# First batch of a sparse-attention and expert kernel: an earlier load, one more query buffer, and a conversion cut in two

## Chip, cores, metric

The kernel runs on one core of a Trainium2 chip. The metric is the device time of one execution in microseconds (us). TensorE (PE) multiplies, VectorE (DVE), ScalarE (ACT) and GpSimd (POOL) do the rest, SyncE (SP) issues most of the loads.

## What is computed

Four batches of attention over 768 positions with 8 heads of 64, in blocks of 32 positions. A query block sees its neighbours, the first and the last block and three sampled blocks; the first and last query block see everything. The 3072 rows of the result go through four experts, weighted by token probabilities.

```python
mask = np.abs(blk_i - blk_j) <= 1
mask = mask | (blk_i == 0) | (blk_j == 0) | (blk_i == n_blocks - 1) | (blk_j == n_blocks - 1)
...
    mask[qb * block:(qb + 1) * block, kb * block:(kb + 1) * block] = True   # sampled blocks
attn = softmax(where(mask, q @ k.T / 8, -1e9)) ; x = attn @ v      # 4 x 8 x 768 x 64
...
p = domain_probs / (domain_probs.sum(-1, keepdims=True) + 1e-09)
for e in range(E):                                                 # 4 experts, 512 -> 1024 -> 512
    h = np.maximum(x @ w1[e], 0.0)
    out += p[:, e:e + 1] * (h @ w2[e])
```

## The kernel before, in words

**Attention units.** A batch is 16 units (`units`, L378): four `Edge` units for the first and last query block, and twelve `Group` units, two for each of six groups of four query blocks (the last group has two blocks). A unit has four steps. `S` computes scores on TensorE, their maxima on VectorE (L266 or L332) and the exponentials on ScalarE (L269 or L337). `T` transposes the probabilities on TensorE (L278) and copies them back on ScalarE (L280). `A` multiplies them with the values (L291) and scales the result on VectorE (L297 to L299). `X`, for the second unit of a group, transposes the result once more (L310) and copies it into the tokens `xr` (L312).

**Loads.** `load_batch` brings keys, `load_q` (L98) the queries of a group, `load_v` (L124) its values (four loads on SyncE, four indirect ones on GpSimd). `copy_k` (L113) copies the edge blocks and the three sampled key blocks of each query block, on GpSimd, ScalarE and VectorE in turn. In the first batch queries have two buffers, values six, which hold the batch's own two tiles and two groups' four.

**The first batch** (loop at L643) is written out by hand, and every engine keeps the order of the program. Step n issues `S` of unit n, `X` of unit n-3, `A` of unit n-2 and `T` of unit n-1; from step 5 on, every second step also issues the loads and copies of the next group but one. Step 9 issues `token_weights` (L619: the load of the expert probabilities, then four small VectorE operations that normalise them) and the first expert weights. From step 11 on each step also takes one piece of weight preparation (`operands`, L446: ScalarE casts to a rounded high part at L464, GpSimd subtracts for the low part at L465), and steps 12 to 15 split a tile of the second weights (L480, L481).

**Conversion.** The expert product works with seven combinations of token quarters, each as a high part (ScalarE cast, L392) and a low part (subtraction on VectorE or GpSimd, L393). `conversion` (L401) makes them in the order 2, 1, 5, 6, 3, 7, 4; four of them need a subtraction on VectorE first (L407, L410, L415, L418). In the first batch 2 and 1 (columns 0 to 383, complete by then) are made at step 12, the five others after the last unit, one ahead of each of the first expert products (L605).

**Expert stream.** `first` (L494) multiplies one combination with a piece of the first weights, six matmuls into PSUM: products 2, 1, 5, 6, 3, 7, 4 in turn, of which 1, 6, 7 and 4 accumulate in one PSUM tile `w` and the others use one tile `v`. ScalarE and VectorE combine the results (L522 to L539). `second` (L542) does the second layer. In the later batches the units are spread through this stream.

Of the kernel before, what the change touches and what calls it, by code (L numbers as in the profile page):

```python
# [8 lines left out]
F32 = mybir.dt.float32  # L9
F32R = mybir.dt.float32r  # L10
# [7 lines left out]
P = 128  # L18
BLOCK = 32
# [4 lines left out]
def attention_moe_kernel(ctx: ExitStack, tc, qb, kb, vr, sampled, sampled_t, probs, w1, w2, out):  # L24


    nc = tc.nc
# [9 lines left out]
    HS = S // 2  # L37
    KH = DM // P // 2
# [5 lines left out]
    QG = P // BLOCK  # L44
    NG = (NB - 2 + QG - 1) // QG
# [4 lines left out]
    xp = ctx.enter_context(tc.tile_pool(name="xp", bufs=1))  # L50
    wp = ctx.enter_context(tc.tile_pool(name="wp", bufs=4))
    at = ctx.enter_context(tc.tile_pool(name="at", bufs=2))
    gp = ctx.enter_context(tc.tile_pool(name="gp", bufs=2))
    ps_at = ctx.enter_context(ExitStack())
    pool = {"s": ps_at.enter_context(tc.tile_pool(name="ps_s", bufs=4, space=PSUM)),
            "a": ps_at.enter_context(tc.tile_pool(name="ps_a", bufs=2, space=PSUM)),
            "o": ps_at.enter_context(tc.tile_pool(name="ps_o", bufs=2, space=PSUM))}
    setup = ctx.enter_context(ExitStack())
    p1 = setup.enter_context(tc.tile_pool(name="p1", bufs=1))
    pool["v"] = setup.enter_context(tc.tile_pool(name="v1", bufs=6))  # L60
    pool["k"] = setup.enter_context(tc.tile_pool(name="k1", bufs=8))

    def f32(ap):
        return ap.bitcast(F32)
# [30 lines left out]
    def blocks(t):  # L95
        return range(1 + QG * t, min(1 + QG * (t + 1), NB - 1))

    def load_q(b, t):  # L98
        js = blocks(t)
        q = gp.tile([P, QG, P], F32, name="q")  # L100
        nc.sync.dma_start(q[:, :len(js)], qb[b, :, js[0]:js[-1] + 1])
        gathered[b, t] = q, {}, {}

# [3 lines left out]
    def sampled_block(j, r):  # L107
        if (j, r) not in regs:
            regs[j, r] = COPIERS[r % len(COPIERS)].value_load(sbrow[:1, j * NR + r, :1],
                                                              min_val=0, max_val=NB - 1)  # L110
        return regs[j, r]

    def copy_k(b, t, cs=range(QG)):  # L113
        for c, j in enumerate(blocks(t)):
            if c in cs:
                k = pool["k"].tile([P, SLOTS - 3, P], F32, name="kr")
                nc.gpsimd.tensor_copy(k[:, :2], keys[b][0][:, 0:NB:NB - 1])
                for r in range(NR):
                    eng = COPIERS[r % len(COPIERS)]
                    copy = eng.copy if eng is nc.scalar else eng.tensor_copy  # L120
                    copy(k[:, 2 + r:3 + r], keys[b][0][:, bass.ds(sampled_block(j, r), 1)])
                gathered[b, t][1][c] = k
# [71 lines left out]
    for r in range(1, NR):  # L194
        for e in range(r):
# [20 lines left out]
    nc.tensor.matmul(mps.rearrange("p t n -> p (t n)"), ind4, sel.rearrange("p t n -> p (t n)"),  # L216
                     start=True, stop=True)
    nc.vector.tensor_copy(mask, mps)

    xr = {}
# [152 lines left out]
    later = {}  # L375
# [11 lines left out]

    xo = {}

    def split(n, src, eng):  # L390
        o = xo[n] = (xp if n in (1, 2) else later["x"]).tile([P, 2, KH, HS], F32R, name=f"xo{n}")
        nc.scalar.copy(o[:, 0], src)  # L392
        eng.tensor_sub(o[:, 1], src, f32(o[:, 0]))  # L393

    def token_blocks(b):
        return [xr[b][:, k * KH:(k + 1) * KH, g * HS:(g + 1) * HS] for k in range(2) for g in range(2)]

    def conversion(b):


        b11, b12, b21, b22 = (xr[b][:, k * KH:(k + 1) * KH, g * HS:(g + 1) * HS]  # L401
                              for k in range(2) for g in range(2))
        split(2, b21, nc.gpsimd)
        yield
        split(1, b11, nc.vector)
        yield
        nc.vector.tensor_sub(b11, b12, b11)  # L407
        split(5, b11, nc.vector)
        yield
        nc.vector.tensor_sub(b11, b22, b11)  # L410
        split(6, b11, nc.vector)
        yield
        split(3, b22, nc.gpsimd)
        yield
        nc.vector.tensor_sub(b12, b22, b12)  # L415
        split(7, b12, nc.vector)
        yield
        nc.vector.tensor_sub(b21, b21, b11)  # L418
        split(4, b21, nc.gpsimd)
        xr.pop(b)  # L420
        yield

    pieces = {}

    def convert(b):
        if b in pieces:
            next(pieces[b], None)
# [188 lines left out]
    pr = const.tile([P, NT // P, E], F32, name="pr")  # L616
    psum_e = const.tile([P, NT // P], F32, name="psum_e")

    def token_weights():  # L619
        nc.sync.dma_start(pr, probs)  # L620
        nc.vector.reduce_sum(psum_e, pr, axis=AX.X)
        nc.vector.tensor_scalar(psum_e, psum_e, 1e-9, None, op0=ALU.add)
        nc.vector.reciprocal(psum_e, psum_e)
        nc.vector.tensor_mul(pr, pr, psum_e.unsqueeze(2).broadcast_to([P, NT // P, E]))
# [3 lines left out]


    with ExitStack() as only:  # L630
        pool["p"] = only.enter_context(tc.tile_pool(name="pp1", bufs=3))
        pool["pt"] = only.enter_context(tc.tile_pool(name="pt1", bufs=2))
        pool["copy"] = nc.vector.tensor_copy
        pool["tag"] = "o"
        pool["xg"] = 1
        load_batch(0)
        load_q(0, 0)
        load_v(0, 0)
        copy_k(0, 0)
        us = units(0)  # L640
        N = len(us)
        E0 = N - 2 * NG
        for n in range(N + 3):  # L643
            if n < N:
                us[n].S()
            if 0 <= n - 3 < N:
                us[n - 3].X()
            if 0 <= n - 2 < N:
                us[n - 2].A()
            if 0 <= n - 1 < N:  # L650
                us[n - 1].T(0)
                us[n - 1].T(1)
            if n == 1:
                load_q(0, 1)
                load_v(0, 1)
                copy_k(0, 1)
            t = (n - E0) // 2
            if n >= E0 and n % 2 and t + 2 < NG:
                load_q(0, t + 2)
                load_v(0, t + 2)  # L660
                copy_k(0, t + 2)

            if n == N - 7:
                token_weights()
                for s in range(2):
                    load_w1(0, s)
                    load_w2(s)
            if n == N - 4:
                pieces[0] = conversion(0)
                convert(0)  # L670
                convert(0)
            if N - 5 <= n < N + 2:
                next(weights)
            if N - 4 <= n < N:
                split_w2(n - N + 4)
# [2 lines left out]
    pool["a"] = pool["o"] = ctx.enter_context(tc.tile_pool(name="ps_a2", bufs=1, space=PSUM))  # L678
    later["m"] = ctx.enter_context(tc.tile_pool(name="ps_m2", bufs=1, space=PSUM))
    setup.close()  # L680
    later["x"] = ctx.enter_context(tc.tile_pool(name="xp2", bufs=1))
    pool["v"] = ctx.enter_context(tc.tile_pool(name="v2", bufs=3))
    pool["k"] = ctx.enter_context(tc.tile_pool(name="k2", bufs=5))
    pool["p"] = ctx.enter_context(tc.tile_pool(name="pp2", bufs=1))
# [3 lines left out]
    later["h"] = ctx.enter_context(tc.tile_pool(name="hp", bufs=2 * FT))  # L688
    later["c"] = ctx.enter_context(tc.tile_pool(name="cp", bufs=2))
    later["o"] = ctx.enter_context(tc.tile_pool(name="op", bufs=KT))  # L690
    convert(0)
    LEAD, TAIL = 12.0, 25.0
    for b in range(1, B):
# [5 lines left out]
        for n in range(N + 1):  # L699
# [12 lines left out]
            if n == 1:  # L712
                copy_k(b, 0)
                load_v(b, 0, (0, 1))
            t = (n - E0 + 2) // 2
            if n % 2 == 0 and 0 < t < NG:
# [54 lines left out]
```

## Time and profile before

| | |
|---|---|
| three runs, us | 1334.69, 1330.58, 1332.21 (median 1332.21) |
| profiled execution, us | 1331.5 |
| its span (first to last instruction), us | 1329.8 |
| mean granted TensorE clock | 0.983 |
| busy share: PE, DVE, ACT, POOL | 94%, 57%, 48%, 51% |
| DMA, mean over the span | 106 GB/s |

A busy share is an average over the whole span; the change touches only the first 120 us of it. The views below are by stretch or in order of time, counted from the span's start. "Idle before, releaser" names the last event that an engine waited for; "issue" stands where the profile shows none. PEclk 1.00 is TensorE's upper level, 2.4 GHz, 0.50 the lower, 1.2 GHz.

### The profile page before, as it was taken

To read this page: it belongs to the slowest core of one execution; us is meant where nothing else is said; L and a number is where in the kernel's file an instruction comes from. 1 tells how busy PE (TensorE), PEld (TensorE's weight loads), DVE (VectorE), ACT (ScalarE), POOL (GpSimd) and SP (SyncE) were. 2 spreads that over 40 slices of the span, in tenths; PEclk is the share of its full clock that TensorE was granted. 3 is DMA by queue.
4 is the path that set the end of the run, shared out by engine and by line. 5 is a ranking of instruction groups with operands and counts; after the bars stand their busy time and mean duration, and the time that the engine had idled before them with its cause. 6 is when DMAs were issued, how large, how long until landed. Compare 5 with 4: busy or idle time off the path is not lost.

```text
span 1329.8 us, 31410 instructions
## 1 busy us (share of the span) xinstructions
PE 1255.4 (94%) x12238; PEld 1079.0 (81%) x12238; DVE 755.5 (57%) x1750; ACT 642.3 (48%) x1678; POOL 675.9 (51%) x872
## 2 busy tenths in 40 slices
PE   7677999999998999999999799999999989999998
PEld 4456888888886778888887688888888778888887
DVE  5476655555556556556545755556555665555553
ACT  4474455555543455555553444555554444444441
POOL 5544555566435455655544543665553464444451
PEclk9898999999998999999999999999999999999999
DMA  8832233353233233444414221444431222222111
GB/s 252 248 117 107 90 96 121 111 151 109 89 112 118 68 96 104 125 128 124 132 62 157 95 72 56 144 122 135 120 107 50 88 79 72 64 64 64 64 48 64
DMA packets 60050, 140.51 MB, mean 106 GB/s; under 512 B 7163, under 2 KB 8700, under 8 KB 59900
## 3 DMA queue, kind: packets, MB, share of 16 engines
q1 hardware_dynamic: 52816, 115.41, 27.6%
q0 software_dynamic: 7040, 23.07, 6.2%
q8 instruction: 96, 1.57, 0.5%
q14 instruction: 54, 0.44, 0.1%
q10 hardware_dynamic: 44, 0.00, 0.0%
HBM read 132.17 MB, written 6.29 MB: 104 GB/s over the span
## 4 chain that ended last, share of the span: by engine, by line
PE 82%; DVE 7%; ACT 4%; DMA 3%; issue 2%; POOL 1%; SPq 1%; DVEq 0%; ACTq 0%
PE po L550 36%; PE w L502 19%; PE v L502 14%; PE o L291 4%; PE tp L278 3%; DMA r<-in_w_dram 2%; PE s L256 2%; PE sw L325 1%; DVE hl L510 1%; PE s L251 1%; DVE oacc L565 1%; DVE xo L393 1%; PE ow L356 1%; ACT hh L509 1%; ACT xo L392 1%
## 5 line engine op out<-in xcount | busy, mean ns | idle before, releaser
L465 POOL TENSOR_TENSOR wo<-r,wo 128x256 fp32r<-128x256 f32 x384 | 301.8, 788 | 411.1 <-ACT wo L464 410.5
L502 PE MATMUL w<-xo,wo 128*128 128x384 f32 x1536 | 316.8, 342 | 14.9 <-DVE z L536 10.9
L550 PE MATMUL po<-h,hh 128*128 128x512 f32 x768 | 312.7, 407 | 7.7 <-DVE oacc L565 7.7
L502 PEld LDWEIGHTS w<-xo,wo 128*128 128x128 f32 x1536 | 276.4, 190 | 39.9 <-DVE z L536 10.9
L550 PE MATMUL po<-h,hl 128*128 128x512 f32 x768 | 305.7, 398 | 0.0
L550 PE MATMUL po<-l,hh 128*128 128x512 f32 x768 | 305.5, 398 | 0.0
L502 PE MATMUL v<-xo,wo 128*128 128x384 f32 x1152 | 238.6, 343 | 12.1 <-ACT p L522 7.9
L464 ACT CAST wo<-r 128x256 fp32r<-128x256 f32 x384 | 153.4, 400 | 181.8 <-DVE r L459 102.9
L502 PEld LDWEIGHTS v<-xo,wo 128*128 128x128 f32 x1152 | 206.8, 190 | 29.3 <-ACT p L522 9.2
L481 POOL TENSOR_TENSOR l<-r,h 128x512 fp32r<-128x512 f32 x128 | 167.6, 1310 | 44.3 <-ACT h L480 44.3
L550 PEld LDWEIGHTS po<-h,hl 128*128 128x128 f32 x768 | 145.4, 189 | 34.0
L550 PEld LDWEIGHTS po<-h,hh 128*128 128x128 f32 x768 | 145.7, 190 | 28.9 <-DVE oacc L565 9.8
L550 PEld LDWEIGHTS po<-l,hh 128*128 128x128 f32 x768 | 146.0, 190 | 14.4
L524 DVE TENSOR_TENSOR p<-w,p 128x384 f32<-128x384 f32 x64 | 35.7, 558 | 166.7 <-PE w L502 163.9
L565 DVE SCALAR_TENSOR_TENSOR oacc<-po,pr,oacc 128x512 f32<-128x512 f32 x168 | 120.3, 744 | 8.1 <-PE po L550 8.0
L269 ACT ACTIVATE p<-p,mx 128x256 f32<-128x256 f32 (+1 forms) x192 | 95.4, 498 | 49.3 <-DVE mx L266 49.3
L136 POOL DMA_INDIRECT v<-in_vr_dram,vidx x88 | 85.0, 966 | 59.4 <-PE o L291 28.4
L465 POOL TENSOR_TENSOR wo<-s,wo 128x256 fp32r<-128x256 f32 x64 | 48.4, 755 | 105.2 <-ACT wo L464 105.2
L266 DVE CUSTOM_DVE_ANT_1 p<-s,mask 128x256 f32<-128x256 f32 (+1 forms) x192 | 69.9, 419 | 56.0 <-PE s L256 56.0
L480 ACT CAST h<-r 128x512 fp32r<-128x512 f32 x128 | 79.2, 619 | 23.0 <-PE po L550 11.6
L510 DVE SCALAR_TENSOR_TENSOR hl<-z,hh 128x384 fp32r<-128x384 f32 x64 | 56.7, 887 | 39.4 <-ACT hh L509 39.4
L509 ACT ACTIVATE hh<-p 128x384 fp32r<-128x384 f32 x64 | 33.6, 525 | 87.5 <-DVE p L524 87.5
(113 smaller groups left out, 1450.5 us busy)
## 6 DMA issues: line engine op xcount, KB each, us to landing
r<-in_w_dram SPq DMA_DIRECT2D x64, 512.0 KB, 3.7
r<-in_w_dram SPq DMA_DIRECT2D x128, 256.0 KB, 2.6
v<-in_vr_dram SPq DMA_DIRECT2D x44, 384.0 KB, 4.7
k<-in_kb_dram SPq DMA_DIRECT2D x8, 768.0 KB, 5.4
out_dram<-oacc SPq DMA_DIRECT2D x24, 256.0 KB, 2.0
v<-in_vr_dram SPq DMA_DIRECT2D x44, 128.0 KB, 4.5
q<-in_qb_dram SPq DMA_DIRECT2D x20, 256.0 KB, 4.1
v<-in_vr_dram SPq DMA_DIRECT2D x4, 1024.0 KB, 9.1
```

The lines of the kernel that those rows point to most:

```text
L136: nc.gpsimd.indirect_dma_start(out=v[:, i, 1], out_offset=None, in_=vr, element_offset=b * S * DM, in_offset=bass.IndirectOffsetOnAxis(ap= ...
L266: nc.vector.tensor_tensor_reduce(p.rearrange("p (a b) -> p a b", b=BLOCK), s[h][:n, i], mk, -SCALE, 3.0e38, ALU.add, ALU.min, mx[:n])
L269: nc.scalar.activation(p, p, AF.Exp, bias=mx[:n], scale=-1.0, accum_out=self.sums[:n, m:m + 1])
L291: nc.tensor.matmul(o[cs, m], self.pt[:, 2 * m + k, cs], vs[c][:, k, e], start=k == 0, stop=k == 1)
L464: nc.scalar.copy(o[:, 0], src)
L465: nc.gpsimd.tensor_sub(o[:, 1], src, f32(o[:, 0]))
L480: nc.scalar.copy(h, r)
L481: nc.gpsimd.tensor_sub(l, r, f32(h))
L502: nc.tensor.matmul(ps, w[:, wi, t], x[:, xi, t], start=fresh and m == 0, stop=m == 3 * KH - 1, skip_group_check=not fresh)
L510: nc.vector.scalar_tensor_tensor(hl, src, 0.0, f32(hh), op0=ALU.max, op1=ALU.subtract)
L550: nc.tensor.matmul(p, a[:, js], w, start=f == 0 and n == 0, stop=f == FT - 1 and n == 2)
L565: nc.vector.scalar_tensor_tensor(accs[tok], p, pe, accs[tok], op0=ALU.mult, op1=ALU.add)
```

## The change

Six edits, all for the first batch. (1) The load of the expert probabilities moves from step 9 to step 3; the normalising operations stay at step 9. (2) Queries get three buffers in the first batch (two afterwards, as before). (3) The block copies of group 0 move behind the scores of unit 0. (4) Probability tiles of the first batch have two buffers instead of three. (5) Combinations 5, 6, 3, 7 and 4 are converted in two parts: columns 0 to 287 of their 384 in steps 16 to 18, right behind `X`, `A` and `T` of the step, and columns 288 to 383 where the whole stood. (6) The memory of the mask tiles is freed once the mask is made, and all `xo` tiles stand in one pool from the start.

```diff
+    pool["q"] = setup.enter_context(tc.tile_pool(name="q1", bufs=3))
+    masks = setup.enter_context(ExitStack())
+    p1 = masks.enter_context(tc.tile_pool(name="p1", bufs=1))
...
-        q = gp.tile([P, QG, P], F32, name="q")
+        q = pool["q"].tile([P, QG, P], F32, name="q")
...
+    masks.close()
...
-    def split(n, src, eng):
-        o = xo[n] = (xp if n in (1, 2) else later["x"]).tile([P, 2, KH, HS], F32R, name=f"xo{n}")
+    def split(n, src, eng, lo=0, hi=HS):
+        if lo == 0:
+            xo[n] = xp.tile([P, 2, KH, HS], F32R, name=f"xo{n}")
+        o = xo[n][:, :, :, lo:hi]
         nc.scalar.copy(o[:, 0], src)
         eng.tensor_sub(o[:, 1], src, f32(o[:, 0]))
...
+    def conversion_early(b):
+        b11, _, b21, _ = halves(b)
         split(2, b21, nc.gpsimd)
         yield
         split(1, b11, nc.vector)
         yield
+    def conversion_late(b, lo=0, hi=HS):
+        b11, b12, b21, b22 = halves(b, lo, hi)
         nc.vector.tensor_sub(b11, b12, b11)
-        split(5, b11, nc.vector)
+        split(5, b11, nc.vector, lo, hi)
...
     def token_weights():
-        nc.sync.dma_start(pr, probs)
...
-        pool["p"] = only.enter_context(tc.tile_pool(name="pp1", bufs=3))
+        pool["p"] = only.enter_context(tc.tile_pool(name="pp1", bufs=2))
...
-        copy_k(0, 0)
         us = units(0)
         N = len(us)
+        CUT = blocks(NG - 1)[0] * BLOCK - HS
...
             if n < N:
                 us[n].S()
+            if n == 0:
+                copy_k(0, 0)
+            if n == 3:
+                nc.sync.dma_start(pr, probs)
...
             if n == N - 4:
-                pieces[0] = conversion(0)
+                for _ in conversion_early(0):
+                    pass
+            if n == N:
+                pieces[0] = conversion_late(0, 0, CUT)
+            if n >= N:
                 convert(0)
                 convert(0)
...
+    pieces[0] = conversion_late(0, CUT)
     convert(0)
```

How the built programs differ in order, at the places that the prediction speaks of (engine rows in the order of execution, without times):

VectorE at the end of the first batch, before: unit 15's scaling (`rec`, `xg`), the copy of the last tokens, and then the conversions (`xr` a subtraction, `xo` a low part).

```order
L297 TENSOR_SCALAR rec<-sums 64x4
L298 RECIPROCAL rec<-rec 64x4
L299 TENSOR_TENSOR xg<-o,rec 64x256
L312 COPY xr<-x 128x4x64
L407 TENSOR_TENSOR xr<-xr 128x2x384
L393 TENSOR_TENSOR xo_2462<-xr,xo_2462 128x768
L410 TENSOR_TENSOR xr<-xr 128x2x384
L393 TENSOR_TENSOR xo_2477<-xr,xo_2477 128x768
```

The same place in the changed program, from the row behind unit 14's scaling.

```order
L414 TENSOR_TENSOR xr<-xr 128x2x288
L398 TENSOR_TENSOR xo_2390<-xr,xo_2390 128x2x288
L417 TENSOR_TENSOR xr<-xr 128x2x288
L398 TENSOR_TENSOR xo_2394<-xr,xo_2394 128x2x288
L300 TENSOR_SCALAR rec<-sums 64x4
L301 RECIPROCAL rec<-rec 64x4
L302 TENSOR_TENSOR xg<-o,rec 64x256
L422 TENSOR_TENSOR xr<-xr 128x2x288
L398 TENSOR_TENSOR xo_2425<-xr,xo_2425 128x2x288
L315 COPY xr<-x 128x4x64
L425 TENSOR_TENSOR xr<-xr 128x2x288
L414 TENSOR_TENSOR xr<-xr 128x2x96
```

Four conversion operations moved ahead of unit 15's scaling and two more ahead of the copy of the last tokens; the pieces of 96 columns follow behind it.

SyncE around the second set of values, before: the query load `q` of group 2 and the loads of its values.

```order
L133 DMA v<-in_vr_dram 32x2x512
L101 DMA q<-in_qb_dram 128x512
L130 DMA v<-in_vr_dram 96x2x512
L133 DMA v<-in_vr_dram 32x2x512
L130 DMA v<-in_vr_dram 96x2x512
```

In the changed program the probabilities' load `pr` stands ahead of that query load; it stood after the fifth set of values.

```order
L135 DMA v<-in_vr_dram 32x2x512
L660 DMA pr<-in_probs_dram 128x96
L103 DMA q<-in_qb_dram 128x512
L132 DMA v<-in_vr_dram 96x2x512
L135 DMA v<-in_vr_dram 32x2x512
```

The query load keeps its row; what changed for it is that no matmul has to free its buffer first.

## Rows read from the trace of the kernel before

**Rows 1.** stretches: busy us of each engine, granted clock, DMA share, GB/s
```profile
62.00:72.00 10.00, 4.99 (x135) 4.26 (x116) 6.11 (x28) 5.30 (x19) 0.97 (x1) 0.50 0.62 221
95.00:106.30 11.30, 4.74 (x24) 4.02 (x24) 7.90 (x9) 4.81 (x9) 3.64 (x4) 1.00 0.96 348
106.30:116.50 10.20, 7.54 (x21) 6.55 (x22) 7.38 (x12) 4.26 (x10) 5.90 (x5) 0.50 0.08 31
116.50:130.00 13.50, 13.50 (x78) 11.21 (x78) 7.86 (x16) 6.20 (x18) 5.30 (x7) 1.00 0.12 41
```

**Rows 2.** the chain of waits up to 125 us: start us, us, what
```profile
55.48 9.06 DMA pr<-in_probs_dram
```

**Rows 3.** VectorE's timeline: start us, us, engine, line, operation, tiles [idle before <-releaser]
```profile
64.56 0.25 DVE L621 TENSOR_REDUCE psum_e<-pr 128x24 f32<-128x96 f32 x1 [7.22 <-DMA pr<-in_probs_dram]
...
65.58 0.42 DVE L266 CUSTOM_DVE_ANT_1 p<-s,mask 128x256 f32<-128x256 f32 x1
```

**Rows 4.** timeline of TensorE, the same columns
```profile
41.62 0.37 PE L251 MATMUL s<-k,q 64*32 64x96 f32 x3 [4.53 <-issue]
...
61.74 0.50 PE L251 MATMUL s<-k,q 64*32 64x96 f32 x16 [2.53 <-issue]
...
68.64 1.93 PE L291 MATMUL o<-v,pt 128*32 128x64 f32 x64 [5.01 <-ACT pt L280]
...
70.50 1.88 PE L278 MATMUL tp<-ident,p 128*128 128x128 f32 x8
...
72.31 0.40 PE L251 MATMUL s<-k,q 64*32 64x96 f32 x16
...
75.06 1.09 PE L278 MATMUL tp<-ident,p 128*128 128x128 f32 x8
```

**Rows 5.** the page: engines (first part) and DMA queues (third part)
```profile
PE 1255.4 (94%) x12238; PEld 1079.0 (81%) x12238; DVE 755.5 (57%) x1750; ACT 642.3 (48%) x1678; POOL 675.9 (51%) x872
q8 instruction: 96, 1.57, 0.5%
```

**Rows 6.** DMA view, queue q8, in 59.0-59.5, 65.5-66.0, 70.5-71.0 us
```profile
q8 instruction: 1, 0.02, 13.0%
q8 instruction: 1, 0.02, 13.1%
q8 instruction: 1, 0.02, 16.5%
```

**Rows 7.** SyncE's waits up to 130 us: waited for, us in total, times, longest
```profile
SPq L101 <- PE s L256: 33.2, 4, 15.6
```

**Rows 8.** timeline up to 15 us, TensorE's first score matmuls, then VectorE
```profile
9.93 2.81 PE L325 MATMUL sw<-k,qe 64*32 64x384 f32 x24
...
10.82 0.33 DVE L121 COPY kr<-k 128x128 f32 x1 [0.58 <-issue]
...
11.61 0.23 DVE L121 COPY kr<-k 128x128 f32 x1 [0.46 <-issue]
```

**Rows 9.** timeline from 95 us: VectorE, ScalarE, GpSimd, TensorE
```profile
97.35 0.96 DVE L393 TENSOR_TENSOR xo<-xr,xo 128x768 fp32r<-128x768 f32 x1 [0.95 <-ACT xo L392]
...
102.22 1.75 DVE L510 SCALAR_TENSOR_TENSOR hl<-p,hh 128x384 fp32r<-128x384 f32 x1 [0.59 <-ACT hh L509]
...
107.14 0.42 DVE L456 TENSOR_TENSOR s<-r 128x256 f32<-128x256 f32 x1
...
96.47 0.84 ACT L392 CAST xo<-xr 128x768 fp32r<-128x768 f32 x1 [2.64 <-issue]
...
100.44 0.41 ACT L464 CAST wo<-r 128x256 fp32r<-128x256 f32 x1
...
101.72 1.83 POOL L393 TENSOR_TENSOR xo<-xr,xo 128x768 fp32r<-128x768 f32 x1
...
95.46 1.31 PE L502 MATMUL v<-xo,wo 128*128 128x384 f32 x6 [0.52 <-DVE xr L312]
...
113.54 2.26 PE L502 MATMUL w<-xo,wo 128*128 128x384 f32 x6 [1.85 <-DVE z L536]
```

More of the change, by code (lines that the diff above doesn't have):

```diff
@@ L58, in attention_moe_kernel @@
     setup = ctx.enter_context(ExitStack())
-    p1 = setup.enter_context(tc.tile_pool(name="p1", bufs=1))
     pool["v"] = setup.enter_context(tc.tile_pool(name="v1", bufs=6))
     pool["k"] = setup.enter_context(tc.tile_pool(name="k1", bufs=8))
+    pool["q"] = setup.enter_context(tc.tile_pool(name="q1", bufs=3))
+    masks = setup.enter_context(ExitStack())
+    p1 = masks.enter_context(tc.tile_pool(name="p1", bufs=1))
     def f32(ap):
@@ L388, in attention_moe_kernel, with halves @@
     xo = {}
-    def split(n, src, eng):
-        o = xo[n] = (xp if n in (1, 2) else later["x"]).tile([P, 2, KH, HS], F32R, name=f"xo{n}")
+    def split(n, src, eng, lo=0, hi=HS):
+        if lo == 0:
+            xo[n] = xp.tile([P, 2, KH, HS], F32R, name=f"xo{n}")
+        o = xo[n][:, :, :, lo:hi]
         nc.scalar.copy(o[:, 0], src)
         eng.tensor_sub(o[:, 1], src, f32(o[:, 0]))
[L395 to L402, printed above, removed]
+    def halves(b, lo=0, hi=HS):
+        return [xr[b][:, k * KH:(k + 1) * KH, g * HS + lo:g * HS + hi] for k in range(2) for g in range(2)]
+    def conversion_early(b):
+        b11, _, b21, _ = halves(b)
         split(2, b21, nc.gpsimd)
@@ L406, in conversion @@
         yield
+    def conversion_late(b, lo=0, hi=HS):
+        b11, b12, b21, b22 = halves(b, lo, hi)
         nc.vector.tensor_sub(b11, b12, b11)
-        split(5, b11, nc.vector)
+        split(5, b11, nc.vector, lo, hi)
         yield
         nc.vector.tensor_sub(b11, b22, b11)
-        split(6, b11, nc.vector)
+        split(6, b11, nc.vector, lo, hi)
         yield
-        split(3, b22, nc.gpsimd)
+        split(3, b22, nc.gpsimd, lo, hi)
         yield
         nc.vector.tensor_sub(b12, b22, b12)
-        split(7, b12, nc.vector)
+        split(7, b12, nc.vector, lo, hi)
         yield
         nc.vector.tensor_sub(b21, b21, b11)
-        split(4, b21, nc.gpsimd)
-        xr.pop(b)
+        split(4, b21, nc.gpsimd, lo, hi)
+        if hi == HS:
+            xr.pop(b)
         yield
+    def conversion(b):
+        yield from conversion_early(b)
+        yield from conversion_late(b)
     pieces = {}
@@ L680, in attention_moe_kernel @@
     setup.close()
-    later["x"] = ctx.enter_context(tc.tile_pool(name="xp2", bufs=1))
+    pool["q"] = ctx.enter_context(tc.tile_pool(name="q2", bufs=2))
     pool["v"] = ctx.enter_context(tc.tile_pool(name="v2", bufs=3))
```

## The prediction

> **What bounds the kernel now.** I read the busy time by stretch first [rows 1]. From 116 us on TensorE sets the pace (busy for all of the 13.5 us shown), and the change moves nothing there. What can be won lies in the first batch, before the steady stream. The stretches from 62 to 72 us and from 106 to 117 us stand out: TensorE is granted 0.50, its lower level of 1.2 GHz, in both, and from 95 to 106 us it is busy for only 4.7 of 11.3 us. The chain of work that ended last then says what the first hole hangs on: 9.06 us of waiting for the load of the expert probabilities [rows 2]. On VectorE the row behind it is the sum over the probabilities, with 7.22 us of idle time ahead of it [rows 3]. VectorE works in order, so the scores' maxima of unit 10 (65.58 us) stand behind that sum; ScalarE's exponentials and its copy of unit 9's transposed probabilities stand behind those, and TensorE gets back to unit 9's output only at 68.64 us, after 5.01 us of waiting for that copy [rows 4].
>
> **A second limit in the same place.** Two of TensorE's waits in that view name no engine but "issue": 4.53 us before 41.62 us, in the middle of one unit's matmuls, and 2.53 us before 61.74 us [rows 4]. I put them down to its instructions coming late. The page counts 12238 matmuls and as many weight loads, and 96 packets of 1.57 MB together on queue q8 of kind "instruction" [rows 5]: 24476 / 96 = 255 instructions and 16 KB per packet. A unit of scores has 64 matmuls and 64 weight loads, a unit of outputs as many, so one packet holds about one unit's work. The DMA view has one such packet starting between 59.0 and 59.5 us, the next between 65.5 and 66.0, the next between 70.5 and 71.0 [rows 6]. TensorE resumed at 61.74 us, some 2.5 us after the first. The block that it entered there holds the scores of unit 11 (128) and the outputs of unit 9 (128), and ends just before unit 10's transposes at 70.50 us. These need the packet of 65.5, and so could not have run before about 65.5 + 2.5 = 68.0 us, whatever VectorE did. The packet of 70.5 began as the block before it was entered; that of 65.5 began some 3.8 us after (61.74), while the DMA engines were loaded (share 0.62 over 62 to 72 us [rows 1]).
>
> **The change part by part.**
> *Probabilities loaded at step 3.* The wait of 7.22 us goes; the four small operations stay (64.56 to 65.58, 1.0 us). VectorE starts unit 10's maxima at 57.3 + 1.0 = 58.4 instead of 65.58. If nothing else were late, everything would move by 7.2 us, which is the one bound. What is late next is the instruction block: unit 11's scores still start at about 61.7, the outputs of unit 9 follow, and the transposes of unit 10 wait until 68.0 instead of 70.50. They take about 1.1 us at the full clock, as at 75.06, instead of 1.88 [rows 4], so unit 12's scores start at about 69.1 instead of 72.31: 3.2 us. The other bound is a second late block: unit 9's outputs end some 5 us earlier, which sets off the last values' load 5 us earlier, into a queue still full of weights. Entered at 68.0 and again late by 3.8 + 2.5, the next block would come at 74.3; what it begins with is now reached just before unit 11's transposes of 75.06: gain about 0.5. I take 3.2 us, one block late by what the trace has shown under load; bounds 0.5 and 7.2.
> The Trainium skill, page "Runtime: NRT & Kernel Launch", section "Instruction fetch mechanics", says that an engine's instructions are refilled in 16 KiB blocks and that crossing a block is mostly hidden. The packet size agrees with the trace; "hidden" does not agree with 4.53 us before 41.62. By that sentence the sum of this part would be the full 7.2 us.
> *Third query buffer.* SyncE waited 33.2 us in four waits for TensorE to free a query buffer [rows 7]. But the value loads queued behind wait for a later release, that of unit 3's, 5's, 7's and 9's outputs, so each query load merely moves ahead of one wait: query 2 among the first loads, query 3 behind the second set of values, and so on. Bytes and order of the rest stay. I put it at 0; each moved load is 256 KB, about 1.2 us at the 221 GB/s of 62 to 72 us [rows 1], so bounds are -1.2 and +1.2.
> *Block copies of the first group behind the first scores.* VectorE's four copies now run under the first score matmuls, the last of them until 11.84 [rows 8]. Of the 24 score matmuls from 9.93 the first eight are unit 0's and end near 10.9, so its maxima can start about 1 us earlier. But the four copies (0.8 us each, as from 10.82 to 11.61) then stand ahead of unit 1's maxima: +3.2 - 1.0 = 2.2 us later. So -1 (if the earlier first unit decides) to +2.2. The 4.53 us before 41.62, if the block comes at its own time, swallow most of it; I take +0.7, a third of the upper end.
> *Two probability tiles instead of three.* A unit's scores on TensorE already stand behind the transposes that free the tile: 0.
> *Conversion of 288 of 384 columns early.* It stands on VectorE behind unit 14's output and ahead of unit 15's. One operation took 0.96 us at 768 elements per partition and 0.42 at 256, on ScalarE 0.84 and 0.41 [rows 9]; that gives 0.76 and 0.69 us for the 576 of the large piece, 0.35 and 0.36 for the 192 of the small one. Ahead of unit 15's scaling now stand two rounds of subtract, cast, subtract: 4 x 0.76 + 2 x 0.69 = 4.4 us. Behind it another round of 2.2 us stands ahead of the copy of the last tokens (L312), which releases the first expert product (0.52 us of waiting before 95.46 [rows 9]). That product starts 4.4 + 2.2 = 6.6 us later. From there to the last product of the first set (113.54) the rest gets shorter: seven VectorE operations by 0.61 each, 4.3 us; three casts that VectorE waits for by 0.48 each, 1.4 us; and the two GpSimd subtractions, 1.83 us now, about a quarter of it then: the operation beside one took 1.75 us on VectorE where a larger one takes 0.96, so 0.8 us back. Sum 6.5. Net +0.1, which I round to 0. Bounds: everything returned and two products freed of the lower clock too (2.26 us for six matmuls at 113.54, half of it at the full clock, so 2.2 us), -2.2; a third returned, +4.4.
> *Sum.* -3.2 + 0 + 0.7 + 0 = -2.5 us. The profiled execution took 1331.5 us (span 1329.8), 0.7 below the median of 1332.2 of the three runs; against the median the forecast is 1329.7.
>
> **The rivals.** A difference under 0.3%, 4 us, is about what a measurement of this kernel cannot tell from none; the forecast lies inside.
> *The whole wait comes back.* Blocks arrive in time once VectorE runs ahead, as the one of 70.5 did. For it: no row of TensorE from 72.31 to 75.06 names "issue". Against it: 4.53 us at 41.62 with no weight load in the queue. Gain 7.2 - 0.7 = 6.5 us: 1325.7. The Trainium skill's sentence above would give this case.
> *The early conversion holds the last unit.* Place: VectorE between unit 14's and unit 15's output. Price: 6.6 us at the first expert product; it decides if the weight work between (its subtractions and casts, in fixed order) and not the conversions sets the pace from there, so that almost nothing is returned. For it: VectorE and GpSimd rows stretch each other [rows 9]. Against it: the conversions, by 6.5 of the 18 us from 95.46 to 113.54, are the largest part of that stretch. Then +6.6 - 2.5 = +4.1: 1336.3, slower; that needs the whole 6.6.
> *The stall only changes its name.* Both blocks come late and the probabilities' wait turns into "issue": -0.5 + 0.7, about 1332.4.
>
> **How the numbers follow.** Forecast 0.44, stall renamed 0.10, both within 0.3%. Whole wait back 0.36, faster. Conversion holds 0.10, slower. The forecast's own range runs from 1327 to 1332. So faster 0.36, same 0.54, slower 0.10. The range leaves out the conversion's case above and some of the fastest below, where half of the conversion's lower bound came on top of the whole wait: 1324.5 to 1334.0.
>
> **What would show it.** Right: the sum over the probabilities has no idle time ahead of it; a wait named "issue" stands before unit 10's transposes, some 3 to 5 us long; unit 12's scores start at 69 to 70 us; the first expert product starts near 99 us (95.5 + 6.6 - 2.5), with the fourth set's product near 111 to 112. Wrong: unit 12's scores at 65 us (whole wait), a first expert product that moved and a last one that did not move back (conversion).

## The result, and the profile after

| | before | after |
|---|---|---|
| median of four runs each, us | 1332.29 (1330.58 to 1334.69) | 1339.6 (1338.0 to 1340.7) |
| ratio, 95% interval | | 1.0057 [1.0044, 1.0071] |
| profiled execution, its span, us | 1331.5, 1329.8 | 1339.52, 1337.8 |
| first matmul of the second layer (`po`), us | 119.2 | 123.8 |
| from there to the last one, us | 1206.4 | 1209.8 |

The kernel became slower by 0.57%, outside the range on record. The span grew by 8.0 us: 4.6 until the second layer begins, and 3.4 in the stream behind it, which the change was not meant to touch.

The stretches of rows 1, after:

```profile
62.00:72.00 10.00, 5.15 (x203) 3.99 (x202) 6.02 (x28) 5.97 (x21) 7.32 (x16) 0.86 1.02 312
95.00:106.30 11.30, 5.01 (x78) 4.01 (x78) 8.57 (x15) 4.92 (x11) 4.92 (x5) 0.57 0.16 48
106.30:116.50 10.20, 8.13 (x32) 7.13 (x33) 7.96 (x16) 4.52 (x12) 5.15 (x7) 0.81 0.88 311
116.50:130.00 13.50, 11.67 (x61) 10.48 (x60) 8.15 (x16) 6.56 (x16) 6.59 (x9) 1.00 0.28 107
```

The first weight loads are issued some 5 us later than before (from 61.2 instead of 56.0 us on), so that they fall into 62 to 72 us and fill the queues there (share 1.02, before 0.62 [rows 1]). Between 116.5 and 130 us TensorE still waits for 1.8 us. The timeline of VectorE shows the sum over the probabilities with no idle time ahead of it, against 7.22 us [rows 3]:

```profile
62.86 0.31 DVE L123 COPY kr<-k 128x128 f32 x1 [0.56 <-issue]
63.01 0.24 DVE L632 TENSOR_REDUCE psum_e<-pr 128x24 f32<-128x96 f32 x1
```

TensorE's timeline shows what took its place: waits named "issue", one of 3.17 us inside unit 9's output, just before unit 10's transposes; further down unit 15's last transposes (103.42), the first expert product, the seventh, and the first matmul of the second layer:

```profile
44.71 0.28 PE L254 MATMUL s<-k,q 64*32 64x96 f32 x4 [3.95 <-issue]
...
56.02 0.51 PE L259 MATMUL s<-kr,q 64*32 64x160 f32 x6 [2.61 <-issue]
...
71.55 0.42 PE L294 MATMUL o<-v,pt 128*32 128x64 f32 x2 [3.17 <-issue]
71.90 1.97 PE L281 MATMUL tp<-ident,p 128*128 128x128 f32 x8
...
78.69 0.43 PE L294 MATMUL o<-v,pt 128*32 128x64 f32 x15 [1.33 <-issue]
...
103.42 0.47 PE L313 MATMUL x<-ident,xg 64*128 64x64 f32 x2 [3.80 <-DVE xg L302]
106.48 2.29 PE L514 MATMUL v<-xo,wo 128*128 128x384 f32 x6 [2.58 <-DVE xr L315]
...
119.14 1.28 PE L514 MATMUL w<-xo,wo 128*128 128x384 f32 x6 [1.70 <-ACT wo L476]
...
123.81 0.39 PE L562 MATMUL po<-h,hh 128*128 128x512 f32 x1
```

Each of the four waits named "issue" ends 2.4 to 2.8 us after a packet of instructions starts in the DMA view: the packets of 41.99, 53.22 and 69.02 us stand ahead of 44.71, 56.02 and 71.55, as that of 59.12 stood ahead of 61.74 in the kernel before. This bears out the prediction's reading of "issue" as instructions that come late.

But the loss begins much earlier. VectorE and TensorE at the start of the changed kernel:

```profile
12.28 0.15 DVE L338 TENSOR_SCALAR mx<-mx 128x1 f32<-128x1 f32 x1
13.42 0.28 DVE L123 COPY kr<-k 128x128 f32 x1 [0.98 <-issue]
...
15.80 0.25 DVE L123 COPY kr<-k 128x128 f32 x1 [0.56 <-issue]
15.97 1.01 DVE L335 TENSOR_REDUCE mx<-sw 128x1 f32<-128x384 f32 x2
...
20.78 1.94 DVE L123 COPY kr<-k 128x128 f32 x1 [0.56 <-issue]
22.64 1.01 DVE L335 TENSOR_REDUCE mx<-sw 128x1 f32<-128x384 f32 x2
```

```profile
25.80 1.51 PE L359 MATMUL ow<-v,ptw 128*32 128x64 f32 x48 [0.99 <-ACT ptw L350]
...
28.71 0.57 PE L254 MATMUL s<-k,q 64*32 64x96 f32 x16
```

Unit 0's maxima end 0.7 us earlier than before, but four copies stand ahead of unit 1's maxima (15.97) and the next group's four ahead of unit 2's (22.64); the last of these takes 1.94 us where the others take 0.23 to 0.43. The scores of unit 4, the first group's, start at 28.71 us; before they started at 24.3.

And in the stream, where both kernels run the same instructions, the expert products became slower. In TensorE's timeline a row of six matmuls of product 6 and the row behind it, of the kernel before and then of the changed one:

```profile
461.37 1.20 PE L502 MATMUL w<-xo,wo 128*128 128x384 f32 x6
462.41 0.40 PE L550 MATMUL po<-h,hh 128*128 128x512 f32 x1
```

```profile
465.64 1.22 PE L514 MATMUL w<-xo,wo 128*128 128x384 f32 x6
466.70 0.39 PE L562 MATMUL po<-h,hh 128*128 128x512 f32 x1
```

From start to start that is 1.04 us before and 1.06 now. Averaged over the trace from 130 us on, successive matmuls of products 5, 6, 3, 7 and 4 start 173.6 to 174.3 ns apart before and 176.6 to 177.1 after; 320 of the 448 products are of these five, 1920 matmuls, and 1920 x 2.8 ns = 5.4 us. Two other steps grew a little, product 2's from 175.7 to 176.9 ns and that of the second layer's 2304 matmuls from 232.8 to 233.3; why, no run shows.

What changed for them is where their tiles lie. Edit 6 puts all `xo` tiles in one pool. In the built programs, the five late token tiles start 64 bytes past a multiple of 512 within a partition before, and on a multiple after; the weight tiles `wo`, and the token tiles of products 2 and 1, start on a multiple in both.

### The profile page after: what moved, and what is told of

It reads as the page before. It is cut to its first block, busy times and chain, and to the rows that moved or that the text cites. A ratio compares the mean times of both kernels' runs of the same rounds, so it can differ in the third digit from the quotient of the medians.

```text
span 1337.8 us, 31424 instructions
## 1 busy us (share of the span) xinstructions
PE 1262.7 (94%) x12238; PEld 1083.2 (81%) x12238; DVE 755.2 (56%) x1757; ACT 644.8 (48%) x1683; POOL 676.4 (51%) x874
## 4 chain that ended last, share of the span: by engine, by line
PE 82%; DVE 8%; ACT 4%; issue 2%; DMA 1%; POOL 1%; DVEq 0%; SPq 0%; ACTq 0%
PE po L562 36%; PE w L514 19%; PE v L514 13%; PE o L294 3%; PE tp L281 3%; PE s L259 2%; PE sw L328 2%; PE s L254 1%; DMA r<-in_w_dram 1%; DVE hl L522 1%; DVE oacc L577 1%; DVE xo L398 1%; ACT hh L521 1%; PE ow L359 1%; ACT xo L397 1%
```

## The experiments

The kernels were timed in four sets (e, f, h and i), each beside the kernel before on the same chip (medians 1332.41, 1332.60, 1331.97 us; 1342.18 in the fourth set, on a chip where all took some 10 us longer). "Second layer" is the start of its first matmul in the profiled execution, "stream" the time from there to its last one, "low" the number of stretches in it in which the granted clock was 0.50 (one of twice the usual length counts as two).

| kernel | median, us | ratio to before, 95% | second layer | stream | low |
|---|---|---|---|---|---|
| before | | | 119.2 | 1206.4 | 6 |
| changed | 1339.6 | 1.0057 [1.0044, 1.0071] | 123.8 | 1209.8 | 3 |
| e1_gap64_late | 1334.7 | 1.0023 [1.0009, 1.0038] | 123.8 | 1206.6 | 6 |
| e2_copies_first | 1337.65 | 1.0051 [1.0033, 1.0070] | 118.7 | 1211.9 | 5 |
| e3_late_whole | 1341.46 | 1.0072 [1.0054, 1.0089] | 124.3 | 1214.2 | 7 |
| e4_probs_only | 1331.82 | 1.0000 [0.9988, 1.0011] | 119.1 | 1206.6 | 6 |
| f1_seven64 | 1330.45 | 0.9988 [0.9972, 1.0004] | 118.6 | 1202.0 | 4 |
| f2_gap_only | 1338.57 | 1.0054 [1.0034, 1.0074] | 124.5 | 1208.9 | 4 |
| f3_best | 1330.27 | 0.9995 [0.9983, 1.0006] | 120.5 | 1203.9 | 5 |
| f4_vector_first | 1339.58 | 1.0064 [1.0043, 1.0086] | 120.8 | 1210.7 | 4 |
| h1_split_loads | 1330.02 | 0.9988 [0.9976, 1.0000] | 117.0 | 1204.0 | 4 |
| h2_before_best | 1328.1 | 0.9978 [0.9967, 0.9988] | 117.1 | 1202.8 | 4 |
| h3_ladder | 1333.04 | 1.0011 [0.9999, 1.0022] | 122.3 | 1205.4 | 4 |
| h4_best_split | 1329.99 | 0.9992 [0.9977, 1.0006] | 119.0 | 1203.8 | 5 |
| i1_copies_gap5 | 1340.43 | 0.9986 [0.9973, 0.9999] | 127.1 | 1208.2 | 5 |
| i2_after_again | 1345.85 | 1.0028 [1.0015, 1.0042] | 127.7 | 1214.0 | 6 |
| i3_copies_again | 1345.48 | 1.0027 [1.0015, 1.0039] | 127.1 | 1214.0 | 6 |

**Where the token tiles lie.** `gap(n, words)` allocates an unused tile of so many 4-byte words per partition. First the five late tiles alone, in the changed kernel; the second gap puts the tiles behind back on a multiple of 512:

```diff
+            if n == 5:
+                gap(0, 16)
             xo[n] = xp.tile([P, 2, KH, HS], F32R, name=f"xo{n}")
+            if n == 4:
+                gap(1, 112)
```

> The changed kernel with 64 bytes of unused memory ahead of the five late token tiles (products 5, 6, 3, 7, 4), so that they start 64 bytes off the multiple of 512 on which the weight pieces start, as they did in the kernel before. Theory (placement): the matmuls of these products return from 176.8 to about 174 ns each, products 2 and 1 stay at 176.7; 1920 matmuls by 2.8 ns give 5.4 us, so about 1334 us. Rival (only the chip or the run differs): no change of the step between matmuls, about 1339.5 us.

The five products went back to 173.7 to 174.1 ns, products 2 and 1 stayed at 175.5 and 176.6, the stream to 1206.6 us, and the median fell by 4.9 us (the ratio from 1.0057 to 1.0023). Product 6 and the row behind it are 1.04 us apart again:

```profile
464.43 1.20 PE L523 MATMUL w<-xo,wo 128*128 128x384 f32 x6
465.47 0.39 PE L571 MATMUL po<-h,hh 128*128 128x512 f32 x1
```

Two gaps of 512 bytes in all, with no instruction changed, give back more than half of the loss. Then the kernel before, with both early tiles moved too:

```diff
+        if n == 2:
+            gap(0, 16)
         o = xo[n] = (xp if n in (1, 2) else later["x"]).tile([P, 2, KH, HS], F32R, name=f"xo{n}")
+        if n == 1:
+            gap(1, 112)
```

> The kernel before, with a gap of 64 bytes ahead of the token tiles xo2 and xo1 and 448 bytes behind them: all seven token tiles then start 64 bytes past a multiple of 512 (before: xo2 and xo1 on a multiple, the other five 64 past one), the weight tiles wo on a multiple as before. Theory (a token tile that starts at the same place modulo 512 as the weights costs 2.8 ns more in each of its 128x384 matmuls): the matmuls of products 2 and 1 fall from 176 to 174 ns, some 1.0 to 2.2 us less in all, 1330.2 to 1331.4 us, and po0 stays at 119.2. Rival (the pace of the stream follows something else, such as the pool's other tiles): products 2 and 1 stay at 176 ns and the time is 1332.4.

All seven now step at 173.2 to 174.2 ns; the stream took 1202.0 us and the median 2.15 us less. The interval reaches 1.0004, so for the total this is likely and not certain; the step itself is plain. Next, is it the tile's own place or its distance from the weights? e1_gap64_late with only its first gap:

```diff
-            if n == 4:
-                gap(1, 112)
```

> The changed kernel with the gap of 64 bytes ahead of xo5 alone, and none behind: xo5 to xo4 start 64 bytes past a multiple of 512, and so do the weights wo and w2's halves; xo2 and xo1 stay on a multiple. If the place of the token tile alone counts, products 5, 6, 3, 7, 4 run at 174 ns and 2 and 1 at 176, and the time is as in the run with both gaps, 1334.7 (1333.5 to 1336). If it is the distance between token tile and weights, the five run at 177 and 2 and 1 at 174: 1338 to 1339.6.

Now weights and late tiles both lie 64 bytes past a multiple of 512. The second alternative came out. TensorE's timeline has product 1, whose tile lies on the multiple, at 1.05 us, and product 6 at 1.07:

```profile
461.23 1.21 PE L521 MATMUL w<-xo,wo 128*128 128x384 f32 x6
462.28 0.40 PE L569 MATMUL po<-h,hh 128*128 128x512 f32 x1
...
466.46 1.23 PE L521 MATMUL w<-xo,wo 128*128 128x384 f32 x6
467.53 0.40 PE L569 MATMUL po<-h,hh 128*128 128x512 f32 x1
```

So the distance counts. Which distances, one run tells with a gap of 64 bytes ahead of every token tile (in e2_copies_first, whose edit follows below):

```diff
+            gap(n, 16)
             xo[n] = xp.tile([P, 2, KH, HS], F32R, name=f"xo{n}")
+            if n == 4:
+                gap(9, 16)
```

> The changed kernel with the first copies back ahead, and 64 bytes between every two token tiles: xo2 starts 64 bytes past a multiple of 512, xo1 128, xo5 192, xo6 256, xo3 320, xo7 384, xo4 448, the weights on a multiple. If only a common start modulo 512 is slow: all seven products at 173 to 174.5 ns, time as with all seven at 64, 1330.3. If the place counts modulo 256 or 128: product 6 (and with 128 also 1 and 7) at 176.5 to 177, the others at 174, 1331 to 1333. If nearness counts (64 being just far enough): 4 slower than the rest.

| bytes past the weights' place (mod 512) | 64 | 128 | 192 | 256 | 320 | 384 | 448 | 0 (changed) |
|---|---|---|---|---|---|---|---|---|
| product | 2 | 1 | 5 | 6 | 3 | 7 | 4 | all |
| ns per matmul | 173.5 | 175.7 | 173.6 | 177.7 | 174.4 | 175.9 | 173.9 | 176.8 |

Every odd multiple of 64 is fast and every multiple of 128 slow, 256 as slow as 0: of the three expectations the second, with the most of it at 256. Apart from 64 and 0, each distance of the table was tried on one product only. That it is the distance and not the product shows from the runs in which all seven products had the same one: there they lie within 1.1 ns of each other (173.2 to 174.2 in f1_seven64, 176.5 to 177.1 in the changed kernel). In the timeline of this kernel product 6 takes 1.06 us and product 3, right behind, 1.05:

```profile
462.27 1.22 PE L522 MATMUL w<-xo,wo 128*128 128x384 f32 x6
463.33 0.39 PE L570 MATMUL po<-h,hh 128*128 128x512 f32 x1
...
464.03 1.21 PE L522 MATMUL v<-xo,wo 128*128 128x384 f32 x6
465.08 0.39 PE L570 MATMUL po<-h,hh 128*128 128x512 f32 x1
```

**The first group's copies.**

```diff
         load_v(0, 0)
+        copy_k(0, 0)
         us = units(0)
...
-            if n == 0:
-                copy_k(0, 0)
```

> The changed kernel with the block copies of group 0 back ahead of the scores of unit 0. Theory (the copies delay units 1 to 4 on VectorE): the first group's scores return from 28.7 to about 24.5 us and the whole gets 3 to 4.5 us faster, about 1335.5 us. Rival (the block fetch sets the time from 41 us on, whatever comes before): the first group's scores return, the scores of unit 8 do not, gain under 1 us, about 1339 us.

Unit 4's scores went back to 24.3 us and the second layer started at 118.7, 5.1 us earlier than in the changed kernel; the median, 1337.65 us, lies between the two expectations. Which engine's copies? VectorE's four alone moved back ahead (`part=0` copies what is VectorE's, `part=1` the rest):

```diff
         load_v(0, 0)
+        copy_k(0, 0, part=0)
...
             if n == 0:
-                copy_k(0, 0)
+                copy_k(0, 0, part=1)
```

> The changed kernel with VectorE's four block copies of the first group back ahead of the first scores, those of GpSimd and ScalarE (and GpSimd's of the edge blocks) behind them as changed. Theory (the cost of the moved copies is VectorE's: its copies stand between the row maxima of units 0, 1 and 2, so the transposes of the first units come late): unit 4's scores at 24.3 to 25.3 instead of 28.7, po0 at 118.7 to 120, total 1334.5 to 1336. Rival (it is the copies of GpSimd and ScalarE, which end late whatever VectorE does, because group 0's gathered scores, or the exponentials on ScalarE, wait for them): unit 4's scores at 27.5 or later, po0 122.5 or later, total 1338 to 1339.6.

Unit 4's scores at 24.4, second layer at 120.8: VectorE's four copies are what delays the head. On this chip f2_gap_only, with all copies behind the scores, began the second layer at 124.5, and f3_best, with all ahead, at 120.5, so VectorE's copies make 3.7 of 4.0 us here. The size is less sure than the 5.1 above: e2_copies_first, f3_best and h3_ladder run the same instructions up to that point and began it at 118.7, 120.5 and 122.3 us. The time that the theory gave did not come: the median stayed at 1339.58 us, and that of e2_copies_first fell only by 2. In the profiled executions their streams were 0.9 and 2.1 us longer than the changed kernel's, with one and two more low stretches. That a faster head costs more of these later is argued, not shown. So both kernels ran once more, in the fourth set:

> The changed kernel with only the first group's copies ahead of the first scores, once more. The first look had the first second-layer matmul 5.1 us earlier than the changed kernel, but the medians only 2 us apart. If 5.1 is the size: second-layer start at 118 to 119.5 again and 1335 to 1336.5 in total. If that look was a lucky head (the next version's was at 120.5): 120 to 121.5 and 1336.5 to 1338. If the stream takes back what the head gains: 118.7 and 1337.7 again.

> The changed kernel once more, beside the two others on one chip: 1339.6 within 1, and a second look at its head: first second-layer matmul at 123 to 124.5. If the first profile was an outlier, the head begins the second layer at 121 or earlier.

On that chip the second layer started at 127.1 against 127.7, and the medians were 0.4 us apart: nothing of what was expected. Part of the reason stands in VectorE's timeline of the kernel with the copies ahead, in the first set and then in the fourth:

```profile
11.75 1.02 DVE L335 TENSOR_REDUCE mx<-sw 128x1 f32<-128x384 f32 x2
12.80 0.16 DVE L337 TENSOR_TENSOR mx<-mx 128x1 f32<-128x1 f32 x1
12.99 0.15 DVE L338 TENSOR_SCALAR mx<-mx 128x1 f32<-128x1 f32 x1
13.06 1.01 DVE L335 TENSOR_REDUCE mx<-sw 128x1 f32<-128x384 f32 x2
14.11 1.30 DVE L337 TENSOR_TENSOR mx<-mx 128x1 f32<-128x1 f32 x1
```

```profile
11.76 0.55 DVE L335 TENSOR_REDUCE mx<-sw 128x1 f32<-128x384 f32 x1
13.05 0.56 DVE L335 TENSOR_REDUCE mx<-sw 128x1 f32<-128x384 f32 x1 [0.75 <-PE sw L328]
13.64 1.76 DVE L337 TENSOR_TENSOR mx<-mx 128x1 f32<-128x1 f32 x1
```

In both, GpSimd makes eight copies one behind the other from 13.6 to 16.0 us. The small operation that joins unit 0's two maxima normally runs ahead of them (12.80, 0.16 us). In the fourth set its second half came 0.75 us late, it fell beside GpSimd's copies and took 1.76 us, and unit 0's transposes began at 16.48 instead of 14.03 us, in the first set and then in the fourth:

```profile
14.03 1.54 PE L349 MATMUL tw<-ident,pw 128*128 128x128 f32 x6 [1.30 <-ACT pw L340]
```

```profile
16.48 1.54 PE L349 MATMUL tw<-ident,pw 128*128 128x128 f32 x6 [3.74 <-DVE mx L335]
```

That is how 0.75 us became 2.45, and one reason why what these copies cost differs between chips: in the changed order unit 0 is safe in both sets (12.28 above, 12.34 in i2_after_again), and what stretches is the copy of 20.78. The Trainium skill, page "GPSIMD Engine Reference", section "1. Specifications", says that GpSimd's way to the on-chip memory is shared with VectorE, with contention for VectorE operations that read two inputs there; the join reads two, and 0.16 against 1.76 us agrees. Why this chip's score half came late (TensorE's scores start at 9.93 us there and at 9.92 in the first set), and why the second layer began 4 and 8 us later there in the two kernels that had run elsewhere, stays open.

**The probabilities.** The kernel before with that load alone moved:

```diff
+            if n == 3:
+                nc.sync.dma_start(pr, probs)
...
     def token_weights():
-        nc.sync.dma_start(pr, probs)
```

> The kernel before with one edit: the load of the expert probabilities at step 3 instead of step 9. Theory (instruction blocks come late and limit the gain): unit 12's scores move from 72.3 to about 69, a wait named issue stands between 62 and 68 us, and the whole gets about 3 us faster, 1329.3 us. Rival (the whole wait comes back): unit 12's scores at 65 us and 1325.5 us.

The ratio is 1.0000: the wait of the theory came, its gain did not. The sum over the probabilities ran at 59.12 us with no idle time, and TensorE then stood still twice:

```profile
67.97 0.27 PE L291 MATMUL o<-v,pt 128*32 128x64 f32 x1 [3.48 <-issue]
68.17 1.97 PE L278 MATMUL tp<-ident,p 128*128 128x128 f32 x8
70.07 0.57 PE L251 MATMUL s<-k,q 64*32 64x96 f32 x16
...
74.83 0.42 PE L291 MATMUL o<-v,pt 128*32 128x64 f32 x14 [1.20 <-issue]
...
76.21 0.40 PE L251 MATMUL s<-k,q 64*32 64x96 f32 x16
```

Unit 12's scores came 2.2 us earlier (70.07), unit 13's not at all (76.21, before 76.1). The packets of instructions started at 65.4 and 72.3 us, 2.5 us ahead of the ends of the two waits; before at 65.6 and 70.7 [rows 6]. The last one got later although the work got earlier. To see whether the weight loads hold it up, two of the four moved two steps back:

```diff
             if n == N - 7:
                 token_weights()
-                for s in range(2):
-                    load_w1(0, s)
-                    load_w2(s)
+                load_w1(0, 0)
+                load_w2(0)
+            if n == N - 5:
+                load_w1(0, 1)
+                load_w2(1)
```

> The kernel before with the probabilities loaded at step 3, as in the run of that part alone, and with two of the four weight loads of step 9 moved to step 11. Theory (the blocks of TensorE's instructions for units 10 and 12 come late since their packets stand behind the weight loads in the DMA engines): no wait of over 1.5 us by 'issue' between 60 and 76 us, unit 12's scores at 67 to 69, unit 13's at 73 to 75, po0 at 116.5 to 118, total 1329 to 1330.5. Rival (the blocks come late for another reason, at the pace at which TensorE uses them up): a wait of 2 to 4 us stays near 65 to 68, unit 13's scores at 76, po0 at 119 and the total at 1331.8 as without the split. Second rival: the later loads meet other transfers and hold up unit 13's or 14's gathered rows, or the second set of products: po0 at 119 or the first products of the second set late, 1332 to 1334.

The second layer started at 117.0 us and the median was 1330.02, as the theory had it, though the interval of the ratio reaches 1.0000. Between 66 and 70 us the stretches show a full DMA side without the split and a light one with it (the rows of e4_probs_only, then h1_split_loads), and the second packet started at 69.3 us instead of 72.3:

```profile
66.00:70.00 4.00, 2.03 (x9) 1.57 (x8) 0.80 (x3) 0.58 (x1) 2.15 (x5) 0.50 1.04 354
```

```profile
66.00:70.00 4.00, 4.00 (x79) 3.24 (x72) 2.58 (x13) 2.66 (x9) 1.51 (x2) 0.50 0.37 100
```

But TensorE's timeline of the split kernel does not look as the theory said:

```profile
64.09 0.58 PE L251 MATMUL s<-k,q 64*32 64x96 f32 x16 [4.04 <-issue]
...
72.98 0.42 PE L291 MATMUL o<-v,pt 128*32 128x64 f32 x14 [0.28 <-issue]
...
74.36 0.40 PE L251 MATMUL s<-k,q 64*32 64x96 f32 x16
```

Unit 12's scores came at 70.0 us as without the split, not at 67 to 69. The wait in unit 9's output is gone, but one of 4.04 us stands ahead of unit 11's scores, behind a stretch that the remaining loads still fill (share 1.04 from 58 to 62 us). Added up between 50 and 80 us, "issue" is 7.9 us without the split and 7.8 with it. What got better is only what follows: unit 13's scores 1.8 us earlier, the second layer 2.1. So the packets follow the load, but that the load makes the waits as a whole is not shown.

**The conversion in two parts.** The late part whole again, behind the last unit:

```diff
-            if n == N:
-                pieces[0] = conversion_late(0, 0, CUT)
-            if n >= N:
-                convert(0)
-                convert(0)
...
-    pieces[0] = conversion_late(0, CUT)
+    pieces[0] = conversion_late(0)
```

> The changed kernel with the late conversion as before: the five late combinations in one piece each, behind the last unit. Theory (the early pieces hold the last unit and return too little): the first expert product comes some 10 us earlier, the fourth of the first set about 3 us earlier, and the whole is about 3 us faster, 1336.5 us. Rival (the conversion is a wash as forecast): within 1 us of the changed kernel, 1339.5 us.

TensorE's first and seventh expert product without the early part:

```profile
100.27 1.31 PE L514 MATMUL v<-xo,wo 128*128 128x384 f32 x6 [0.51 <-DVE xr L315]
...
118.30 2.26 PE L514 MATMUL w<-xo,wo 128*128 128x384 f32 x6 [1.85 <-ACT wo L476]
```

The early part delays the first product by 6.2 us (106.48) and gives back 5.4 by the seventh (119.14) and the rest by the second layer, 123.8 against 124.3. The medians differ by 1.9 us in its favour, with intervals that overlap: the theory is out, and the rival (no difference) is not told from a small gain.

**Together.** First the changed kernel without the two costs found, that is with the edits of e1_gap64_late and e2_copies_first:

> The changed kernel with the two suspected costs taken out and nothing else: the first group's copies ahead of the first scores, and the five late token tiles 64 bytes past a multiple of 512 as before. If the two account for the whole loss (probabilities, query buffer and early conversion worth 0 together): 1332 within 1.5, the time of the kernel before. If a third cost remains: 1334 or more. If the early parts do gain once these two are out: 1330 or less.

With a ratio of 0.9986 [0.9973, 0.9999] no third cost remains. Against i3_copies_again, from which it differs by the gaps alone, it took 5.0 us less: on this chip, where the changed kernel lost 3.7 us, the placement alone is more than the whole loss. The next three look for a version that beats both kernels: all seven tiles moved and the copies ahead, in the changed kernel; then the same with the loads split; and the kernel before with early probabilities, split loads and seven tiles moved.

> The changed kernel with the first group's block copies back ahead of the first scores, and all seven token tiles 64 bytes past a multiple of 512 (weights on a multiple). If the two costs add (5.1 us of copies up to the first second-layer matmul, 2.8 ns in each of 1920 matmuls and something in the 768 of products 2 and 1): po0 at 118.7, products at 174 ns, and 1328 to 1330.5 us, faster than the kernel before by 2 to 4. If they don't add (the five products of the last part then wait for something else): 1332 to 1335.

> The changed kernel with the first copies back ahead, all seven token tiles at 64, and two of the four weight loads at step 11 instead of 9. If the loads delay TensorE's blocks: the waits of 4.4 us before 65.7 and 1.5 before 75.4 shrink to under 1.5 each, po0 falls from 120.5 to 117 to 119, total 1327 to 1329. If not: 1330.3 as without the split.

> The kernel before with three things: probabilities at step 3, the weight loads split over steps 9 and 11, and all seven token tiles 64 bytes past a multiple of 512. If the split brings 2 us and the placement 2: 1328 to 1329, faster than before by 3 to 4.5. If the split brings nothing: 1330.4 as with the placement alone.

The changed kernel mended reached 1330.27 us (0.9995), at the upper end of what was expected, its second layer at 120.5 instead of 118.7. With the split it began at 119.0, but the wait ahead of unit 11's scores stayed (4.16 us before 64.22) and the median fell by 0.3 us only. Both are level with before. The one that is faster than both is h2_before_best, 1328.1 us and 0.9978 [0.9967, 0.9988], built on the kernel before: it has none of the early conversion, the third query buffer or the moved copies.

## Why the prediction was wrong

*"The change moves nothing there"*, of the stretch from 116 us on. This step failed, and it is the largest. The stream from 116 us on has the same instructions, but the pool's new layout put five token tiles at a distance from the weights that costs 2.8 ns in each of 1920 matmuls: 5.4 us worked out, 4.9 and 5.0 measured. The rows of the kernel before could have raised the question, since products 2 and 1 stepped at 176 ns beside 174 for the others.

*"Block copies of the first group behind the first scores", +0.7.* Wrong in size. It measured +5.1 at the start of the second layer on one chip (e2_copies_first), +4.0 on a second, of which VectorE's copies make 3.7, and +0.6 on a third; by the medians it is between 0 and 2 us. Its upper end was 2.2. The term weighed the four copies against unit 1's maxima and had that about right, but looked no further: the next group's four follow, and unit 2's maxima then come at 22.64 instead of 19.2 us. And it assumed that the "issue" wait near 42 us would swallow most of it; the wait moved along (44.71).

*"Probabilities loaded at step 3", -3.2.* The working found the right limit and stopped one block early. The block for unit 10's transposes came late as described (3.17 us after, 3.48 alone, resuming at 67.97 where 68.0 was worked out). The transposes behind it still ran at the lower clock, 1.97 us where 1.1 was taken, so unit 12's scores came at 70.07 instead of 69.1. Then the next block was late too, the case at the other bound, a gain of 0.5 us and "the stall only changes its name": measured 0. The Trainium skill's sentence that a block boundary is mostly hidden (page "Runtime: NRT & Kernel Launch", section "Instruction fetch mechanics") is not what these rows show.

*Third query buffer, probability tiles, 0.* Not tried alone; with both in it, i1_copies_gap5 left no loss to explain.

*"Conversion of 288 of 384 columns early", 0.* Right, mechanism and size: 6.6 us later forecast and 6.2 measured at the first product; 6.5 forecast back by the seventh product, 5.4 measured there and 6.7 by the second layer. The rival that the early part holds the last unit fell.

*The signs on record.* Two came: no idle time ahead of the sum over the probabilities, and 3.17 us of "issue" before unit 10's transposes. Two did not: unit 12's scores at 73.80 us instead of 69 to 70, and the first expert product at 106.48 instead of 99, behind a head that the copies had made late. With the copies ahead (e2_copies_first) unit 12's scores did come at 69.83.

*The sum.* At the second layer, by one profile each: copies +5.1, probabilities -0.1, conversion -0.5, together +4.5 against +4.6 measured. That it meets so well is in part luck, since the same head began the second layer anywhere from 118.7 to 122.3 us. In the stream the steps of all seven products add up to 6.1 us more, and 0.5 ns in each second-layer matmul to 1.1 us; three low stretches fewer gave some 3.9 back (an estimate: from e4_probs_only to h1_split_loads, with the tiles in the same place, two fewer went with 2.6 us less stream). That makes +3.3, against 3.4 measured, and 8.0 measured with the head; the medians moved by 7.3. The range, up to 1334.0, had no term for the stream. The upper ends of its four terms together (-0.5 + 1.2 + 2.2 + 4.4 = +7.3 against the median) would have come to 1339.5, near the result, but for other reasons than those measured.

## What to carry to other kernels

Look up where tiles start when a change touches pools: an edit that moves no instruction can change the pace of every matmul that reads a moved tile, and two small gap tiles show it in one run. When a stall is lifted, follow the work to the second limit behind it, not only the first. Cheap copies on an in-order engine are priced by everything that follows them until the queue has caught up, and by what the neighbouring engine does meanwhile.

## What the runs showed of the hardware

This kernel's 128x384 matmul steps at 173 to 175 ns when its token tile starts an odd multiple of 64 bytes from the place of its weights (modulo 512), and at 175.4 to 177.7 when it starts a multiple of 128 away, 256 and 0 being the worst; 128, 192, 256, 320 and 384 were seen in one run only (h3_ladder). The Trainium skill, page "TensorE: Matmul & The Clock Gate", section "Step-by-step: what each phase is for", says that loading the next weights takes no read bandwidth from the running matmul, which reads through a port of its own; by that the place of the weights would not be expected to matter. In f2_gap_only the slow products changed with it, so the measurement differs. What makes the 2 to 4 ns, and whether the weight load takes part in it, no run here shows.

A VectorE operation of 0.16 us took 1.30 to 1.76 beside GpSimd's copies, so a lateness of 0.75 us became 2.45.
